# An inverse transform over 64 frequencies as three products of split float32r operands instead of one fp32 product

## The chip, the cores and the metric

The kernel runs on one core of a Trainium2 chip. The metric is the device time of one execution in microseconds; before the change the median of three runs is 1478.95 us (1478.46 to 1480.79).

## The reference

The input x has 8 batches of 2496 rows by 256 features. Each batch goes through a real Fourier transform along the rows, a complex 256 x 256 linear layer with bias, a soft threshold, and the inverse transform. The rows of all batches (19968) then go through a mixture of eight experts, each of which takes exactly 2496 rows, chosen greedily by the order of all logits:

```python
X = np.fft.rfft(x, axis=1);  Xr, Xi = X.real, X.imag
Yr = Xr @ w_r - Xi @ w_i + b_r
Yi = Xr @ w_i + Xi @ w_r + b_i
Y  = soft(Yr, 0.01) + 1j * soft(Yi, 0.01)      # sign(v) * max(|v| - 0.01, 0)
y  = np.fft.irfft(Y, n=2496, axis=1)
# gate: logits = y @ w_gate; pairs (row, expert) in falling order, a row goes to
# the first expert that still has room (2496 rows each)
out[rows of e] = np.maximum(y[rows of e] @ w1[e], 0) @ w2[e]
```

## The kernel before

The transform of length 2496 = 39 x 64 is done in two steps, forward and back. For one batch these are: a transform over 39 points (matmuls of L1168), a change of layout through a scratch tensor T1 in DRAM, the transform over 64 points (L1208), the linear layer (L1227 for the two outputs' own terms, L1235 for the shared one, with the weights as split pairs), bias and soft threshold on VectorE and ScalarE (L1238 to L1246), the inverse over 64 frequencies (L1256), a way through T2 in DRAM, the inverse over 39 (L1294, in the last batch L1287), and the transposes and the gate's products for the logits (L1314, L1336). The frequencies of one batch go in ten groups p = 0 to 9.

Most of the products are made of split operands: a float32 value is rounded to a float32r "high" part and the rest is subtracted out as a "low" part, and high x high, high x low and low x high are summed in PSUM as three float32r products. The inverse over 64 frequencies is one of those that are not: `mm4` (from L1251) multiplies plain fp32. For two groups p at once it does eight matmuls, each over 64 rows (one of the halves i of the partitions, a row tile of TensorE) by 256 columns; the halves write two PSUM tiles `ps4`. In the profile a plain fp32 matmul is two records. Its moving operand is y after the threshold, its weights are the tiles `Gt` (constant cG, 20 blocks of 128 x 128, loaded once at the start).

The tiles live in rings (`RINGS`): a name with so many buffers. y has three (`y1`), the threshold's helper t one (`y2`); after the threshold y lies in `y1` until `mm4` has read it. After the transform stage the same buffers are lent to the experts by the lists `G2` and `GROUPS`: `W`, the experts' split weights, lies in `sp8`, `sh8` and `FG8`.

The order of all instructions is written in advance by a planner (`Plan.run`): every task has an engine, a duration, a place `pos` and the tasks it depends on; the planner plays the work through and gives each engine the task that can start first, with `pos` to decide between tasks that are ready within a small hold time. Constants `Q` shift the places, `SLACK` adds safety to waits, `port=True` marks VectorE and GpSimd tasks that the planner keeps from overlapping. The batches overlap: while one is in its middle, the next is in its first transform and the last in its second.

From the logits of the first four batches VectorE makes the lists of 512 rows for each of eight "early" blocks (`Router.early`), which TensorE starts on while the last batches are still running; the closing rounds (`Router.closing`) then fill up the experts one after the other, and each round's list is needed by the block of 1984 rows that follows (`Experts.run`; L710 first product, L729 and L730 second; L535 writes the list, L657 gathers the rows, L742 scatters the results, L683 writes the split, turned rows).

Of the kernel before, what the change touches and what calls it, by code (L numbers as in the profile page):

```python
# [280 lines left out]
P1X = -8.145  # L281
LATE = dict(sp=1.71, raw=7.61, gather=2.51, scatter=6.24)
SLACK = dict(split=1.661, count=0.243, back=0.303, lists=0.8, os=1.437, hid=0.28, mm4=0, mm4l=0.807, tr=0.477, trl=2.345, gate=0.682, gatel=2.407)
IOTA = True
Q = dict(hV=0.086, hA=0.014, hT=0.054, hP=0.38, e0=43.3, e1=87.756, en=112.714, le=5.187, ge=4.634, c0=1028.809, cs=55.92, c1=1077.612, c1a=1056.826, n0=223.981, n2=109.946, ll=69.251, gs=66.402, gl=3.358, be=14.243, bl=76.075, xp=17.572, f0=8.116, p1=-0.114, p1s=0.45, p57=2.954, p57s=0.337, p5=3.739, p56s=1.261, p5s=0.966, xl=3.918, xs=1.11, m2=0.077, m3=-0.909, zz=2.417, m4=-0.514, l5=4.692, s5=-1.867, w5=1.439, t5=1.266, g5=-3.412, r0=12.442, gb=0.7, gw=0.71, lg=1.866, aa=0.168, ba=3.378, sc=3.601, k2=2.568, xw=1.4, xv=4.054, xv2=2.336, gl2=13.031)
YLV = (1, 5, 7)
SOFT = (2, 3, 4, 5, 6)
# [29 lines left out]
class Kit:  # L317
# [675 lines left out]
def phase_a(K, H, x, w_r, w_i, b_r, b_i, w_gate, cD1, cF, cG, cD5, YD, LG, NB=B):  # L993
# [17 lines left out]
    Gt = [sb("FG8" if b - a > 4 else "FG2", [128, b - a, 128]) for a, b in CUT]  # L1011
# [9 lines left out]
    def dve(n): return 0.068 + n / 960  # L1021
# [51 lines left out]
    def load_weights(after):  # L1073
# [38 lines left out]
    def batch(b):  # L1112
# [22 lines left out]
        if b: T1 = K.dram("T1", [128, 20, 256])  # L1135
        else: Z = [sb(k, [128, 2, b1 - a1, 128]) for k, (a1, b1) in zip(("sp8", "sp8", "xt"), SH)]
# [61 lines left out]
        zs, zd = [], []  # L1198
        for p in range(10):
# [58 lines left out]
            gates['mm4', b, p][0] = plan.add('T', 2.12, pos + Q['m4'], mm4, zs + zd + [BG_[part(GQ, 2 * p)]], list(ps4), uses=[Gt[p // 8]], slack=SLACK['mm4l' if b == NB - 1 else 'mm4'])  # L1258
# [4 lines left out]
            zs, zd = [], []  # L1263
# [84 lines left out]
    last_sh, yt, yq = [], [], []  # L1348
# [7 lines left out]
def fast(tc, nc, H, x, w_r, w_i, b_r, b_i, w_gate, cD1, cF, cG, cD5, YD, LG, w1, w2, cR, out, spectral=True):  # L1356

    RINGS = dict(xt=2, xh=2, xl=2, s1st=3, sh8=4, sh4=2, FG8=2, FG2=2, sp8=2, yr=2, xTh=2, xTl=2, y1=3, y2=1, s4st=2, s2c=3, s2h=2, s2l=2, yst=3, yTh=5, yTl=4, lgst=1,
# [251 lines left out]
```

## Time and profile before

| | |
|---|---|
| median of three runs | 1478.95 us |
| the profiled execution, its span | 1477.74 us, 1475.9 us |
| mean granted TensorE clock | 0.997 of full speed |
| busy of the span: TensorE, VectorE, ScalarE, GpSimd | 98%, 77%, 60%, 36% |
| transfers | 240.50 MB, mean 163 GB/s |
| lines of the inverse over 64 (L1256) | 640 matmul records, 80.6 us |
| of the linear layer (L1227) | 960 matmul records |

A busy share is the time in which the engine has at least one instruction running. TensorE's matmuls overlap, so the sum of their durations is more than the busy time, and how far apart they start tells more of their cost than how long one takes. The transform stage with its tail ends at about 585 us, where the last logits are computed; the experts' products begin at 537 us and run to the end.

### The profile page before, as it was taken

The page shows a single profiled execution, that of the slowest core. Times are in us where ns is not written, and L with a number is a line of the kernel's source. Part 1 is how long each engine was busy: PE and PEld are TensorE (multiplying, and loading weights), DVE is VectorE, ACT ScalarE, POOL GpSimd, SP SyncE. Part 2 cuts the span into 40 slices and gives each one's busy share as a digit, 9 for nine tenths or more (in the row PEclk, how much of TensorE's full clock was granted, in tenths as well). Part 3 has the DMA queues.
Part 4 walks back from the last instruction along what each step waited for, and adds up shares of the span by engine and source line. Part 5 has one row for each costly group of instructions (what it writes and reads, how often), then busy time and mean ns, then how long its engine had stood idle before and what let it go on. Part 6 is the DMA issues. An engine that isn't in the chain of part 4 may idle for free.

```text
span 1475.9 us, 32728 instructions
## 1 busy us (share of the span) xinstructions
PE 1449.2 (98%) x9135; PEld 1221.8 (83%) x9142; DVE 1131.0 (77%) x3234; ACT 888.7 (60%) x2092; POOL 525.2 (36%) x497
## 2 busy tenths in 40 slices
PE   8999999999999999999999999999999999999997
PEld 7888888888888877888878878788888888888886
DVE  6868788875899888899999898997877554553432
ACT  4678999999899786444546363645446542442331
POOL 0013414343432543521444535445453535321112
PEclk9999999999999999999999999999999999999999
DMA  5697869787777656433543536354434334321000
GB/s 199 205 316 247 281 213 293 226 283 231 232 231 251 205 172 193 159 119 104 169 136 110 169 109 180 123 161 138 133 118 141 113 118 143 113 67 42 24 22 30
DMA packets 221994, 240.50 MB, mean 163 GB/s; under 512 B 97598, under 2 KB 183787, under 8 KB 221803
## 3 DMA queue, kind: packets, MB, share of 16 engines
q1 hardware_dynamic: 201833, 180.00, 39.2%
q0 software_dynamic: 19840, 58.22, 12.0%
q8 instruction: 74, 1.21, 0.3%
q14 instruction: 117, 0.96, 0.2%
q10 hardware_dynamic: 130, 0.11, 0.0%
HBM read 139.34 MB, written 98.91 MB: 161 GB/s over the span
## 4 chain that ended last, share of the span: by engine, by line
PE 85%; DVE 7%; ACT 3%; DMA 2%; issue 2%; SPq 1%; POOL 0%; POOLq 0%; DVEq 0%; ACTq 0%
PE b L710 23%; PE b L729 15%; PE b L730 8%; PE b L1227 7%; PE b L1256 5%; PE b L1208 4%; PE b L1235 4%; PE b L1168 3%; PE b L1294 3%; PE pt L710 3%; PE pt L729 2%; PE b L1314 2%; PE pt L730 1%; PE b L732 1%; PE b L1336 1%
## 5 line engine op out<-in xcount | busy, mean ns | idle before, releaser
L1038 POOL TENSOR_TENSOR s2l<-s2c,s2h 120x512 fp32r<-120x512 f32 (+1 forms) x84 | 105.0, 1256 | 257.9 <-ACT s2h L1035 246.9
L1227 PE MATMUL b<-wt,xTh 128*128 128x256 f32 x640 | 128.3, 297 | 0.9 <-ACT xTh L1214 0.9
L742 POOL DMA_INDIRECT out_dram<-xTh,li x64 | 65.2, 1018 | 158.5 <-DVE xTh L739 97.5
L1227 PEld LDWEIGHTS b<-wt,xTh 128*128 128x128 f32 x640 | 103.1, 191 | 6.5 <-issue 1.4
L742 POOL DMA_INDIRECT out_dram<-xTl,li x64 | 66.0, 1032 | 101.8 <-DVE xTl L739 56.9
L1325 POOL TENSOR_TENSOR yTl<-yr,yTh 128x468 bf16<-128x468 f32 (+1 forms) x55 | 61.3, 1115 | 102.5 <-ACT yTh L1321 79.1
L1208 PE MATMUL b<-FG,sh 128*128 128x128 f32 x640 | 92.2, 278 | 1.2 <-DVE sh L1189 1.2
L1227 PE MATMUL b<-wt,xTl 128*128 128x256 f32 x320 | 91.9, 287 | 1.3 <-DVE xTl L1217 1.3
L1208 PEld LDWEIGHTS b<-FG,sh 128*128 128x128 f32 x640 | 82.7, 191 | 6.3 <-issue 2.4
L738 ACT COPY xTh<-b 128x256 f32<-128x256 f32 x66 | 24.7, 374 | 95.2 <-PE b L730 76.6
L1256 PE MATMUL b<-y,FG 64*128 64x256 f32 x640 | 80.6, 390 | 0.1
L1240 DVE TENSOR_TENSOR y<-b,sx 128x512 f32<-128x512 f32 x80 | 54.9, 688 | 27.1 <-ACT sx L1238 24.2
L1256 PEld LDWEIGHTS b<-y,FG 64*128 64x128 f32 x640 | 58.3, 186 | 12.8 <-issue 1.3
L1168 PE MATMUL b<-xh,d 117*120 117x512 f32 (+1 forms) x154 | 64.2, 423 | 2.3 <-ACT xh L1035 2.2
L1294 PE MATMUL b<-s2h,d 120*117 120x512 f32 (+1 forms) x168 | 65.9, 399 | 0.0
L1319 DVE TENSOR_TENSOR yr<-b,yTh 128x468 f32<-128x468 f32 (+1 forms) x88 | 54.8, 625 | 13.9 <-ACT yTh L1318 13.0
L1038 DVE TENSOR_TENSOR xl<-xt,xh 117x512 fp32r<-117x512 f32 (+1 forms) x77 | 56.8, 747 | 11.0 <-ACT xh L1035 10.7
L1235 PE MATMUL b<-wt,xTh 128*128 128x256 f32 x320 | 63.4, 291 | 0.0
L1227 PEld LDWEIGHTS b<-wt,xTl 128*128 128x128 f32 x320 | 60.8, 190 | 3.1 <-DVE xTl L1217 2.7
L634 POOL DMA_INDIRECT xt<-in_moe_w_dram,wi x32 | 33.8, 1055 | 67.6 <-DVE sh L644 20.7
L738 ACT COPY xTl<-b 128x256 f32<-128x256 f32 x68 | 25.4, 373 | 53.8 <-PE b L730 39.9
L739 DVE TENSOR_TENSOR xTh<-b,xTh 128x256 f32<-128x256 f32 x66 | 27.6, 418 | 38.8 <-ACT xTh L738 36.4
(1229 smaller groups left out, 5275.1 us busy)
## 6 DMA issues: line engine op xcount, KB each, us to landing
T<-s4st SPq DMA_DIRECT2D x80, 256.0 KB
s2c<-T SPq DMA_DIRECT2D x80, 240.0 KB
YD<-yst SPq DMA_DIRECT2D x80, 234.0 KB
xt<-in_x_dram SPq DMA_DIRECT2D x35, 512.0 KB
sh<-T SPq DMA_DIRECT2D x35, 512.0 KB
T<-s1st SPq DMA_DIRECT2D x70, 240.0 KB
xt<-in_moe_w_dram SPq DMA_DIRECT2D x32, 512.0 KB
XG<-yTh SPq DMA_DIRECT2D x11, 256.0 KB
```

The lines of the kernel that those rows point to most:

```text
L710: T.matmul(ps.t[:, 0:w], lhsT=W1[m].t[:, a, 128 * ft:128 * ft + 128], rhs=x_.t[:, 0:w], start=q + m == 0, stop=q + m == 3)
L729: T.matmul(ps.t, lhsT=hh.t[:, u:u + 128], rhs=W2[ft // 4].t[:, :, ft % 4], start=ft == 0, stop=False)
L730: T.matmul(ps.t[:, 0], lhsT=hl.t[:, u:u + 128], rhs=w_[0], start=False, stop=ft == 7)
L742: ins = P.indirect_dma_start(out=self.out, out_offset=bass.IndirectOffsetOnAxis(ap=oi.t[0:M, oo + t:oo + t + 1], axis=0), in_=o.t[0:M], in ...
L1038: lambda: eng.tensor_tensor(lb[1](), src(), hb[1](), op=OP.subtract), [srcb, hb[0]], [lb[0]], port=True)
L1168: T.matmul(ps.t[0:M], lhsT=d1[0:k_, a, 0:M], rhs=v.t[0:k_], start=i == 0, stop=i == 2)
L1208: T.matmul(ps.t[:, :, dt, i], lhsT=sh[k // 8].t[:, k % 8, 128 * dt:128 * dt + 128], rhs=at(Ft, k), start=True, stop=True)
L1227: T.matmul(pc.t[:, c], lhsT=a.t[:, 1 - c, dt], rhs=wt[2 - c].t[:, w, dt], start=not pb and dt == 0 and a is th and w == 0, stop=(c == 1 or ...
L1235: T.matmul(pa.t, lhsT=a.t[:, 2, dt], rhs=wt[0].t[:, w, dt], start=dt == 0 and a is th and w == 0, stop=dt == 1 and a is tl)
L1256: T.matmul(ps4[i].t[:, r], lhsT=at(Gt, 2 * (p - 1 + r) + c)[h], rhs=zs[r].t[h, c], start=c == 0, stop=c == 1)
L1294: T.matmul(ps.t[0:M, gs_], lhsT=d5[0:k_, a, 0:M], rhs=v.t[0:k_, gs_], start=i == 0, stop=i == 2)
L1325: yq.append(plan.add('V' if on else 'P', dve(2 * W) if on else pool(2 * W), pos + Q['t5'], lambda yh=yh, yl=yl, yr=yr, W=W, on=on: (V if o ...
```

## The change

In batches 1 to 7 (batch 0 stays in fp32) the value z after the threshold is split on the way: a copy rounds it into `zh` (VectorE, float32r), and a subtraction leaves the rest in `zl` (VectorE for odd p, GpSimd for even p). `mm4x` then does three float32r products, G high x zh, G low x zh and G high x zl, 24 matmuls where there were eight. The constant cG holds G and its two float32r parts side by side, and `load_g` brings the parts in by six transfers from GpSimd's queue in the first batch; the high part takes the two `sp8` tiles, the low part follows in the tiles of the fp32 constant. z is written to `zl`'s ring (batch 0) or in place of t, y's ring has one buffer, and the planner's constants `Q`, `SLACK` and `P1X` have other values throughout.

```diff
-    return dict(cD1=two(D1), cF=Fm.astype(np.float32), cG=G.astype(np.float32), cD5=two(D5))
+    return dict(cD1=two(D1), cF=Fm.astype(np.float32), cG=np.concatenate([G, split(G)[0], split(split(G)[1])[0]], axis=1).astype(np.float32), cD5=two(D5))
...
-P1X = -8.145
+P1X = -9.506
...
+ZLV = (1,)
...
-    Gt = [sb("FG8" if b - a > 4 else "FG2", [128, b - a, 128]) for a, b in CUT]
+    Gt = [sb("G8" if b - a > 4 else "G2", [128, b - a, 128]) for a, b in CUT]
...
+            GH[:] = sb("sp8", [128, 16, 128], F32R), sb("sp8", [128, 8, 256], F32R)
+            GL[:] = sb("G8", [128, 16, 128], F32R), sb("G2", [128, 4, 128], F32R)
...
             y, t, zz = sb("y1", [128, 2, 256]), sb("y2", [128, 2, 256]), vb()
+            z = t if b else sb("zl", [128, 2, 256])
...
-                plan.add('V', dve(512), pos + Q['zz'], lambda y=y, t=t: V.scalar_tensor_tensor(y.t, y.t, 0.0, t.t, op0=OP.min, op1=OP.add), [y, t], [y, zz], port=True)
+                plan.add('V', dve(512), pos + Q['zz'], lambda y=y, t=t, z=z: V.scalar_tensor_tensor(z.t, y.t, 0.0, t.t, op0=OP.min, op1=OP.add), [y, t], [z, zz], port=True)
...
+            if b:
+                zh, zl, zq = plan.buf("zh", lambda s: GH[1].t[:, 2 + 2 * int(s[2:]):4 + 2 * int(s[2:])]), sb("zl", [128, 2, 256], F32R), vb()
+                plan.add('V', dve2(512), pos + Q['zz'], lambda z=z, zh=zh: V.tensor_copy(zh.t, z.t), [zz, BH_[-1]], [zh, zq], uses=[z, GH[1]], port=True)
+                on = p % 2 in ZLV
+                plan.add('V' if on else 'P', dve(512) if on else pool(512), pos + Q['zz'], lambda z=z, zh=zh, zl=zl, on=on: (V if on else P).tensor_tensor(zl.t, z.t, zh.t, op=OP.subtract), [zq], [zl], uses=[z, zh, GH[1]], port=True)
+                z, zz = zl, zl
+                zu.append(zh)
...
+            def mm4x(p=p, zs=zs, zu=zu, ps4=ps4):
+                for r in range(2):
+                    for c in range(2):
+                        k = 2 * (p - 1 + r) + c
+                        for n, (g, z) in enumerate(((ghi(k, 1)[:, 0], zu), (GL[k // 16].t[:, k % 16], zu), (ghi(k, 1)[:, 0], zs))):
+                            for i in range(2):
+                                h = slice(64 * i, 64 * i + 64)
+                                T.matmul(ps4[i].t[:, r], lhsT=g[h], rhs=z[r].t[h, c], start=c == n == 0, stop=c == 1 and n == 2)
...
+        if not b: load_g(ev)
...
+    def load_g(ev):
+        for q, (k0, k1) in enumerate(GQ):
+            G, o = k0 // 16, k0 // 16 * 16
+            add_dma(10 + Q['gs4'], lambda k0=k0, k1=k1: nc.gpsimd.dma_start(ghi(k0, k1 - k0), cG[:, 20 + k0:20 + k1].bitcast(F32R)), 65e3 * (k1 - k0), [], [GH[G], BH_[q]], 'P', after=ev[:1], run=512 * (k1 - k0))
+            add_dma(10 + Q['gs4'], lambda k0=k0, k1=k1, G=G, o=o: nc.gpsimd.dma_start(GL[G].t[:, k0 - o:k1 - o], cG[:, 40 + k0:40 + k1].bitcast(F32R)), 65e3 * (k1 - k0), [], [GL[G], BL_[q]], 'P', after=fg[1], run=512 * (k1 - k0))
...
-    RINGS = dict(... FG8=2, FG2=2, sp8=2, ... y1=3, y2=1, ...
+    RINGS = dict(... FG8=1, FG2=1, G8=1, G2=1, sp8=2, zh=3, ... y1=1, y2=1, zl=2, ...
```

## Rows read from the trace of the kernel before

**Rows 1.** The page: busy us (share) xinstructions, and granted clock in 40 slices

```profile
PE 1449.2 (98%) x9135; PEld 1221.8 (83%) x9142; DVE 1131.0 (77%) x3234; ACT 888.7 (60%) x2092; POOL 525.2 (36%) x497
...
PEclk9999999999999999999999999999999999999999
```

**Rows 2.** The chain of waits from 200 to 300 us: start us, us, what

```profile
by line: PE b L1227 24.3%; PE b L1168 15.2%; PE b L1208 13.8%; PE b L1256 13.5%; PE b L1294 12.5%; PE b L1235 11.4%; PE b L1314 6.5%; PE b L1336 2.9%
...
208.83 1.93 PE b L1256 x16
210.75 1.62 PE b L1227 x12
...
218.96 1.43 PE b L1227 x12
...
250.07 1.93 PE b L1256 x16
```

**Rows 3.** TensorE's waits from 95 to 568 us: us in total, times, longest

```profile
PE pt L471 <- DVE cnt L466: 1.8, 2, 1.1
```

**Rows 4.** Busy time of each engine by stretch, with instructions, clock, transfers

```profile
core 0: us, PE busy (x) PEld busy (x) DVE busy (x) ACT busy (x) POOL busy (x), PEclk, DMA share, GB/s
95.20:568.00 472.80, 466.82 (x3738) 397.95 (x3743) 390.49 (x826) 417.67 (x954) 178.31 (x152) 1.00 0.76 242
421.30:485.70 64.40, 63.51 (x535) 54.62 (x535) 60.93 (x180) 58.99 (x145) 19.20 (x15) 1.00 0.74 240
568.00:706.00 138.00, 138.00 (x784) 113.61 (x783) 125.75 (x420) 69.39 (x170) 43.81 (x42) 1.00 0.38 125
0.00:95.20 95.20, 87.38 (x615) 74.77 (x616) 70.64 (x179) 57.34 (x133) 0.70 (x6) 0.98 0.69 230
```

**Rows 5.** Line L1256 (ns min/median/max), and one task of it in the timeline

```profile
L1256 PE MATMUL b<-y,FG x640: 376/376/480, 37.7 to 531.3; 64*128 64x256 f32 x160
...
250.00 2.00 PE L1256 MATMUL b<-y,FG 64*128 64x256 f32 x16
...
250.00 1.60 PEld L1256 LDWEIGHTS b<-y,FG 64*128 64x128 f32 x16
...
250.00 0.19 PEld L1256 LDWEIGHTS b<-y,FG 64*128 64x128 f32 x2
```

**Rows 6.** Lines of the nearest operations: ns min/median/max, first and last start, forms

```profile
L1245 DVE TENSOR_SCALAR y<-y x30: 394/421/1400, 31.4 to 528.3; 128x512 f32<-128x512 f32 x30
...
L1246 DVE TENSOR_TENSOR y<-y,y x30: 675/688/1751, 32.3 to 528.7; 128x512 f32<-128x512 f32 x30
...
L1038 POOL TENSOR_TENSOR s2l<-s2c,s2h x84: 727/1284/1754, 96.8 to 535.8; 120x512 fp32r<-120x512 f32 x70, 120x256 fp32r<-120x256 f32 x7, 40x256 fp32r<-40x256 f32 x7
...
L1038 DVE TENSOR_TENSOR xl<-xt,xh x77: 674/684/1766, 25.6 to 427.1; 117x512 fp32r<-117x512 f32 x70, 78x512 fp32r<-78x512 f32 x7
...
L1218 DVE TENSOR_TENSOR xTl<-sx,xTh x80: 402/417/1514, 26.5 to 523.7; 128x256 fp32r<-128x256 f32 x80
```

**Rows 7.** VectorE and GpSimd in the timeline around 245 us: start us, us

```profile
244.26 0.69 DVE L1229 TENSOR_TENSOR b<-b,bf 128x512 f32<-128x512 f32 x1
244.86 0.42 DVE L1215 TENSOR_TENSOR sx<-b,sx 128x256 f32<-128x256 f32 x1
...
246.39 1.08 DVE L1218 TENSOR_TENSOR xTl<-sx,xTh 128x256 fp32r<-128x256 f32 x1
...
246.11 1.08 POOL L1325 TENSOR_TENSOR yTl<-yr,yTh 128x468 bf16<-128x468 f32 x1
```

**Rows 8.** Groups by line and shape, 0 to 1050 us: busy us, mean ns of one

```profile
L1038 DVE TENSOR_TENSOR xl<-xt,xh 117x512 fp32r<-117x512 f32 x70 | 52.0, 753 | 9.5 <-ACT xh L1035 9.5
...
L1218 DVE TENSOR_TENSOR xTl<-sx,xTh 128x256 fp32r<-128x256 f32 x80 | 40.7, 509 | 0.7 <-ACT xTh L1216 0.5
```

**Rows 9.** The first closing expert in the timeline: list's waiter, its rows, first product

```profile
706.47 0.98 POOL L742 DMA_INDIRECT out_dram<-xTh,eoi  x1 [3.29 <-DVE li L535]
...
736.38 0.68 DVE L683 TENSOR_TENSOR s2l<-yTl,FG 128x512 fp32r<-128x512 f32 x1
...
745.59 0.40 PE L710 MATMUL b<-s1st,sp 128*128 128x512 f32 x1
```

More of the change, by code (lines that the diff above doesn't have):

```diff
@@ L280 @@
 UX = 6
[L281 removed]
+P1X = -9.506
 LATE = dict(sp=1.71, raw=7.61, gather=2.51, scatter=6.24)
[L283 removed]
+SLACK = dict(split=1.232, count=0.28, back=0.343, lists=0.657, os=2.117, hid=0.956, mm4=0.318, mm4l=0.855, tr=0.555, trl=2.378, gate=0.645, gatel=2.461)
 IOTA = True
[L285 removed]
+Q = dict(hV=0.085, hA=0.009, hT=0.041, hP=0.322, e0=45.966, e1=88.74, en=107.337, le=8.978, ge=-3.041, c0=1027.621, cs=56.794, c1=1078.68, c1a=1064.524, n0=191.639, n2=95.971, ll=48.387, gs=72.789, gl=2.94, be=14.728, bl=69.672, xp=19.043, f0=8.429, p1=-0.156, p1s=0.45, p57=1.995, p57s=1.281, p5=3.533, p56s=1.457, p5s=0.966, xl=4.239, xs=0.81, m2=-0.131, m3=-0.467, zz=1.197, m4=-3.175, l5=5.748, s5=-1.157, w5=1.781, t5=1.367, g5=-1.587, r0=11.753, gb=0.7, gw=0.71, lg=1.288, aa=0.264, ba=2.517, sc=2.914, k2=2.829, xw=4.354, xv=3.181, xv2=1.704, gl2=12.612, gs4=0.482)
 YLV = (1, 5, 7)
+ZLV = (1,)
 SOFT = (2, 3, 4, 5, 6)
@@ L1078, in load_weights @@
         for i, w in enumerate((w_r, w_i)):
-            st = sb("y1", [128, 2, 256])
+            st = sb("y2" if i else "y1", [128, 2, 256])
             sw.append(st)
@@ L1135, in batch @@
         if b: T1 = K.dram("T1", [128, 20, 256])
-        else: Z = [sb(k, [128, 2, b1 - a1, 128]) for k, (a1, b1) in zip(("sp8", "sp8", "xt"), SH)]
+        else:
+            Z = [sb(k, [128, 2, b1 - a1, 128]) for k, (a1, b1) in zip(("sp8", "sp8", "xt"), SH)]
+            GH[:] = sb("sp8", [128, 16, 128], F32R), sb("sp8", [128, 8, 256], F32R)
+            GL[:] = sb("G8", [128, 16, 128], F32R), sb("G2", [128, 4, 128], F32R)
         for u in range(NU):
@@ L1197, in batch @@
         T2 = K.dram("T2", [128, 20, 256])
-        zs, zd = [], []
+        zs, zd, zu = [], [], []
         for p in range(10):
@@ L1256, in mm4 @@
                             T.matmul(ps4[i].t[:, r], lhsT=at(Gt, 2 * (p - 1 + r) + c)[h], rhs=zs[r].t[h, c], start=c == 0, stop=c == 1)
+            def mm4x(p=p, zs=zs, zu=zu, ps4=ps4):
[6 more added lines that the diff above has]
+                                T.matmul(ps4[i].t[:, r], lhsT=g[h], rhs=z[r].t[h, c], start=c == n == 0, stop=c == 1 and n == 2)
             gates['mm4', b, p] = [0]
-            gates['mm4', b, p][0] = plan.add('T', 2.12, pos + Q['m4'], mm4, zs + zd + [BG_[part(GQ, 2 * p)]], list(ps4), uses=[Gt[p // 8]], slack=SLACK['mm4l' if b == NB - 1 else 'mm4'])
+            gates['mm4', b, p][0] = plan.add('T', 1.5 if b else 2.12, pos + Q['m4'], mm4x if b else mm4, zs + zd + zu + [X[part(GQ, 2 * p)] for X in ((BH_, BL_) if b else (BG_,))], list(ps4), uses=[GL[p // 8], GH[p // 8], GH[1]] if b else [Gt[p // 8]], slack=SLACK['mm4l' if b == NB - 1 else 'mm4'])
             for i in range(2):
@@ L1346, in batch, with ghi @@
             ys = []
-    last_sh, yt, yq = [], [], []
+    last_sh, yt, yq, GH, GL = [], [], [], [], []
+    BH_, BL_ = [vb() for _ in GQ], [vb() for _ in GQ]
+    def ghi(k, n):
+        return GH[0].t[:, k:k + n] if k < 16 else GH[1].t[:, k // 2 - 8:(k + n + 1) // 2 - 8].rearrange("p a (c m) -> p (a c) m", c=2)[:, k % 2:k % 2 + n]
+    def load_g(ev):
[3 more added lines that the diff above has]
+            add_dma(10 + Q['gs4'], lambda k0=k0, k1=k1, G=G, o=o: nc.gpsimd.dma_start(GL[G].t[:, k0 - o:k1 - o], cG[:, 40 + k0:40 + k1].bitcast(F32R)), 65e3 * (k1 - k0), [], [GL[G], BL_[q]], 'P', after=fg[1], run=512 * (k1 - k0))
     head, wl, fg = [], [], []
```

14 lines of the change are left out of this document (7 added, 7 removed).

## The prediction, made before the result was known

> **What bounds the kernel now.** I read the page first, then the chain of waits in one stretch, then TensorE's waits, then the busy times by stretch. On the page TensorE is busy 98% of the span at full clock, VectorE 77% [rows 1]. A busy share alone doesn't say that an engine is the bound, so the chain comes next: between 200 and 300 us every link of it is TensorE, with no other engine and no transfer in it [rows 2]. The list of waits agrees: from 95 to 568 us, the seven batches that the change touches and the first expert work, TensorE's largest wait for another engine sums to 1.8 us [rows 3]. So a microsecond taken off TensorE there is a microsecond off the kernel, as long as something else is not late. What would be late next is read from the same stretch: VectorE is busy 390.5 of 472.8 us, ScalarE 417.7, GpSimd 178.3, and in its fullest batch (421.3 to 485.7) VectorE was busy 60.9 of 64.4 us, 95% [rows 4].
>
> **TensorE: eight steps become twelve shorter ones.** One task of the inverse (two frequencies' pairs) is now 8 matmuls, each recorded as two, so 16 records, and in the chain it costs 1.93 us each time; the twelve L1227 matmuls behind it take 1.62 us where they take 1.43 elsewhere, so some 0.19 us more for the change of row tiling and back [rows 2]. That part stays, as the new products use the same two 64-row tiles. The records go in pairs, one in each half of the rows: the timeline has two weight loads within 0.19 us, as long as one. The first pair starts at 250.00 and waits about 0.10 for weights (480 against 376 ns), the last begins at 252.00 - 0.38 = 251.62, so the seven steps between take (251.62 - 250.10) / 7 = 0.217 us each [rows 5]. Eight steps are 1.74 us.
>
> The new task has 24 matmuls, three for each of the eight, all float32r over 256 columns: twelve pairs. No row of before has a float32r pair in two row tiles. The nearest is float32r of the same 256 columns over all rows: twelve L1227 in 1.43 us, 0.12 each [rows 2]. If a pair again costs what one costs, twelve are 1.44 us, and a task gains 0.30 (0.296 unrounded). Seven batches have five tasks each: 35 x 0.296 = 10.4 us; I use 10.2, as the rows are rounded. Bounds: at best a step is half of the present one (0.108), which gives 1.30 per task and 35 x 0.44 = 15.4 us; at worst the halves don't pair in float32r, 24 x 0.12 = 2.88, and the change costs 35 x 1.14 = 40 us. I take 0.12, as the pairing in the trace is one of tiles, not of a data type.
>
> The row first: sixteen weight loads of 64 x 128 were issued within 1.60 us, two at a time [rows 5]. The Trainium skill ("TensorE: Matmul & The Clock Gate", LDWEIGHTS (loading the stationary operand)) says that a load's time goes by its columns, not its rows, about 107 ns for 128. By that alone, one load after the other, 24 loads would be 2.57 us by estimate, and the change would lose (rival D). The Trainium skill ("TensorEngine Tiling (Array Packing)", Key Properties) lets different tiles load in parallel, and the trace agrees with that one.
>
> **VectorE and GpSimd: the two new passes.** Per frequency pair p there is now a copy of z to its rounded half (VectorE) and a subtraction that gives the rest, on VectorE for odd p and on GpSimd for even p. So each of the 35 tasks adds two copies and one subtraction to VectorE, and one subtraction to GpSimd. The nearest copy is L1245, 512 elements in SBUF with one operand, 421 ns; the subtraction is L1246, 688 ns, and on GpSimd L1038, 1284 ns [rows 6]. On a filled VectorE the next instruction starts before the last has ended: from 244.26 to 244.86, 0.60 us after one of 0.69 [rows 7]. I take 0.08 off each: 2 x 0.34 + 0.61 = 1.29, times 35 = 45 us on VectorE (from both sides: 33 if a copy took half as long, 54 with the full durations) and 35 x 1.28 = 45 us on GpSimd, which goes from 178 to 223 of 472 and has room.
>
> A second cost comes with it. VectorE's L1218 at 246.39 took 1.08 us instead of 0.417, and ended just after GpSimd's L1325, which ran from 246.11 to 247.19 [rows 6, 7]: an operation with both inputs in SBUF waited for GpSimd. The means show its size: L1218 509 against 417 ns, 80 times, and L1038 on VectorE 753 against 684, 70 times: 7.4 + 4.8 = 12.2 us [rows 6, 8], 15% of their 81 us. With a quarter more GpSimd work, these rise by some 3 us, and the new 54 us of VectorE operations, all between SBUF tiles, pay 15% x 1.25, 10 us: 13 us more (0 if the written order keeps them apart, 25 if it is twice as bad). The Trainium skill ("SBUF — State Buffer", Who interferes with whom) calls this an exclusive lock that also holds for copies in the two-port mode; the trace agrees for two SBUF inputs, and L1245 (maximum 1400 ns) fits for one. By that lock the other way round GpSimd too would wait for the copies, which moves nothing, as it has room.
>
> **What is late next.** VectorE's work from 95.2 to 568 becomes 390.5 + 45 + 13 = 448.5 us. TensorE would need 472.8 - 10.2 = 462.6 us for it; that is a VectorE filled to 97%. The fullest batch reached 95% with TensorE hardly waiting [rows 3, 4]. At 95% the stretch takes 472.1, at 94% 477.1, at 93% 482.3 us. VectorE does not hold each batch back at once, since the routing of the early experts is loose work that slides. Where the delay comes due is the first closing expert: its list is there by 706.47, its gathered rows, turned and split, at 736.38 + 0.68 = 737.06, and its first product runs at 745.59 [rows 9], 8.5 us of margin, with VectorE 91% busy from 568 to 706 [rows 4]. TensorE comes 10.2 us earlier, the rows come L later or earlier than now, so TensorE waits max(0, 1.7 + L). Later closings have more.
>
> I take a fill of 94.5%, a little under what the fullest batch had: 474.6 us, L = 1.8, wait 3.5, net 10.2 - 3.5 = 6.7 us.
>
> **What I cost at nothing.** The two more copies of the inverse's constants are 40 x 64 KB = 2.6 MB over six GpSimd issues: at the 230 GB/s of 0 to 95.2, 11 us of transfers, in a stretch where the transfers' engines are 69% busy and GpSimd works 0.7 us [rows 4]; they must be there at the second batch's first task, at 95 us. Uncovered, up to 11 us. z, now kept in two more buffers while y keeps one: the buffers' count is the same, and TensorE's task waits for a subtraction 1.7 us later than before. Behind it in TensorE's order stand other products of the same and the next batch, whose evictions all engines wait for; the order is written for it, so nothing, and at worst one wait like the longest now (1.1 us, rows 3) at each task, 38 us. The planner's constants are all moved, and with them the order of everything: TensorE waits so little that a better order has some 2 us to give [rows 3], and a worse one is priced in C. The first expert's weights lose two tiles that were free since the first batch: these now hold constants until the last task (529 us); two to four splits later, TensorE has the last batch's tail to do. Nothing, up to 5 us.
>
> **The sum.** 1477.74 us for the profiled execution (span 1475.9 and 1.84 around it) less 6.7 is 1471.0; the median of the runs lies 1.2 above the profiled one, so 1478.95 - 6.7 = **1472 us**.
>
> **Rivals.**
> A, all of it arrives: VectorE fills to 97% or GpSimd's lock costs nothing, so no wait at the first closing expert: 1478.95 - 10.2 = 1469, and 1463.5 with the step of 0.108. For it: 95% was reached with TensorE untouched. Against: only in one batch, with routing work that nobody waited for.
> B, VectorE takes it all back: fill 93% gives L = 9.5, wait 11.2, net -1: 1480, no change.
> C, slower: VectorE becomes the bound of the seven batches. The point is a fill of 92.6% (L = 11.5, net -3). At 92%, 487.5 us, L = 14.7, wait 16.4: net -6.2, 1485; at 91%, 1490. For it: over the whole stretch VectorE is at 83% now. Against: in most of that stretch it waits because TensorE hands it nothing.
> D, the change doesn't do what it says on TensorE: float32r in two row tiles doesn't pair, matmuls or loads come one after the other, +40 us, 1519. Only a missing row speaks for it; the paired loads speak against.
>
> **How the numbers follow.** The forecast (net 3 to 9.5) has 0.41, A 0.17, B 0.15, C 0.23, D 0.04. A measurement of this kernel can tell about 0.2% (3 us) from no change: faster 0.41 + 0.17 = 0.58, same 0.15, slower 0.27. The forecast's own range is 1469.5 to 1476. For 8 in 10 I go from A's lower end, 1463, to C at 91.5%, 1487; outside lie D and the worst of C and of the uncovered waits.
>
> **What would show it.** Right: a task of the inverse at 1.60 to 1.68 us in the chain (1.93 now), its loads still two at a time; VectorE busy 93% or more from batch 2 to 7; a TensorE wait of a few us around the first closing expert, or a list that comes before 706. Wrong: a task near 3 us (D); VectorE's new copies far from 0.34 to 0.42 us; TensorE waiting for the new subtraction at every task; or idle VectorE together with an unchanged time.

## The result: slower by 1.4%

The changed kernel takes 1499.63 us (median of 4 runs, 1496.98 to 1501.41), the kernel before 1478.7 beside it: 1.0138 times as long (95% interval 1.0119 to 1.0157). The prediction was 1472, range 1463 to 1487; the slower side is what happened, and by more than rival C priced it. The profiled execution took 1499.81 us with a span of 1498.0, 22.1 more than before. Lines are a few numbers higher than before: the inverse's product is L1277 (L1256 before), the new copy L1254, the new subtraction L1256, the linear layer L1231 and L1239, its input's low parts (xTl) L1221 and L1222.

From the page of the changed kernel, to compare with [rows 1]: busy times, VectorE's slices, the clock's slices, and the engines' shares of the chain that ended last (for each instruction, followed back, what released it):

```profile
PE 1448.8 (97%) x9418; PEld 1227.7 (82%) x9422; DVE 1196.0 (80%) x3339; ACT 886.9 (59%) x2092; POOL 589.8 (39%) x538
...
DVE  6869998988899999899999889989877655554431
...
PEclk9999999999999989999999999999999999999999
...
PE 80%; DVE 13%; ACT 3%; issue 2%; DMA 1%; POOL 0%; SPq 0%; POOLq 0%; DVEq 0%; ACTq 0%
```

The busy shares alone hardly differ. In the chain, though, VectorE's share is twice that of the kernel before:

```profile
PE 85%; DVE 7%; ACT 3%; DMA 2%; issue 2%; SPq 1%; POOL 0%; POOLq 0%; DVEq 0%; ACTq 0%
```

Where the time went is seen in one stretch, from the second batch's first task of the inverse to the last product of the logits. Its busy times by engine (as [rows 4]), in the kernel before:

```profile
95.20:585.10 489.90, 483.92 (x3868) 410.95 (x3875) 406.07 (x877) 427.02 (x987) 186.38 (x159) 1.00 0.75 240
```

and in the changed kernel:

```profile
100.80:609.40 508.60, 481.15 (x4142) 414.02 (x4146) 465.66 (x979) 426.95 (x992) 238.52 (x193) 0.99 0.74 229
```

The stretch starts 5.6 us later, is 18.7 us longer, and 2.2 us come back behind it: 22.1. TensorE's busy time falls by 2.8 us only, and its idle time (the stretch less the first number, PE) rises from 6.0 to 27.5. VectorE rises from 406.1 to 465.7, 83% to 91.6%.

TensorE's waits from 100 to 600 us in the changed kernel (total, times, longest), the six largest, to compare with [rows 3], where the largest was 1.8:

```profile
PE b L1231 <- DVE xTl L1221: 7.0, 7, 1.7
PE pt L811 <- DVE rng L888: 4.9, 1, 4.9
PE b L1172 <- DVE xl L1039: 2.7, 5, 0.8
PE b L1239 <- DVE xTl L1222: 2.6, 4, 1.1
PE b L1277 <- DVE sp L1254: 2.2, 1, 2.2
PE b L1316 <- DVE cnt L466: 1.9, 1, 1.9
```

All six end with VectorE, but hardly any with the new passes: TensorE waits mostly for older work (xTl, xl, the lists) that now comes later in VectorE's order. The waits are not spread evenly. The stretch in five parts (columns as above):

```profile
100.80:280.00 179.20, 172.20 (x1499) 151.87 (x1500) 165.45 (x289) 154.78 (x342) 81.66 (x63) 1.00 0.80 248
280.00:400.00 120.00, 119.84 (x1074) 106.17 (x1075) 101.16 (x176) 111.02 (x246) 66.81 (x54) 1.00 0.84 262
400.00:490.00 90.00, 79.88 (x674) 68.98 (x672) 88.51 (x256) 72.06 (x165) 33.27 (x27) 0.98 0.60 190
490.00:540.00 50.00, 49.98 (x470) 45.14 (x471) 48.28 (x107) 38.81 (x97) 26.41 (x21) 1.00 0.51 157
540.00:609.40 69.40, 59.25 (x440) 41.85 (x438) 62.26 (x156) 50.28 (x146) 30.36 (x30) 0.93 0.74 222
```

TensorE is idle 7.0 us, 0.2, 10.1, 0.0 and 10.2, with VectorE busy 92%, 84%, 98%, 97% and 90%. So a full VectorE does not by itself stop TensorE; which pass is late, and what waits for it, must count too. How one wait comes about is seen around 271 to 277 us, here ordered by cause:

```profile
270.82 1.36 POOL L1347 TENSOR_TENSOR yTl<-yr,yTh 128x468 bf16<-128x468 f32 x1 [3.80 <-ACT yTh L1343]
271.16 1.57 DVE L1256 TENSOR_TENSOR zl<-y,sp 128x512 fp32r<-128x512 f32 x1
272.76 0.73 ACT L1247 ACTIVATE y<-y,ml 128x512 f32<-128x512 f32 x1 [0.57 <-DVE zl L1256]
...
275.59 1.22 POOL L1347 TENSOR_TENSOR yTl<-yr,yTh 128x468 bf16<-128x468 f32 x1 [1.72 <-ACT yTh L1343]
275.80 1.29 DVE L1222 TENSOR_TENSOR xTl<-sx,xTh 128x256 fp32r<-128x256 f32 x1
277.15 0.39 PE L1239 MATMUL b<-wt,xTl 128*128 128x256 f32 x1 [1.06 <-DVE xTl L1222]
```

The new subtraction takes 1.57 us in place of 0.68, as GpSimd's L1347 runs until 272.18. ScalarE's next threshold (L1247) waits 0.57 us for it. ScalarE's later work, xTh among it, stands behind that, and VectorE's xTl, made from xTh, is itself held by the next L1347 of GpSimd and takes 1.29 us in place of 0.42. TensorE then waits 1.06 us. The chain that ended last runs through all of these VectorE passes, where it stayed on TensorE for 100 us on end before [rows 2]. The Trainium skill ("SBUF — State Buffer", Who interferes with whom) calls the hold an exclusive lock; the trace agrees.

The largest single wait, 4.9 us from 548 to 553, is neither for xTl nor for a new pass. Ahead of rng in VectorE's order stand two passes of the experts' weights' split (L645, median 0.68 us each), which took 5.90 us together while four passes of GpSimd ran:

```profile
547.07 5.90 DVE L645 TENSOR_TENSOR sh<-xt,sh 128x512 fp32r<-128x512 f32 x2
547.26 2.12 POOL L1347 TENSOR_TENSOR yTl<-yr,yTh 128x468 bf16<-128x468 f32 x2
549.32 2.48 POOL L1039 TENSOR_TENSOR s2l<-s2c,s2h 120x512 fp32r<-120x512 f32 x2
```

### The profile page after: what moved, and what is told of

It is laid out like the page before. It is cut to its first block, busy times and chain, and to the rows that moved or that the text cites. A ratio compares the mean times of both kernels' runs of the same rounds, so it can differ in the third digit from the quotient of the medians.

```text
span 1498.0 us, 33534 instructions
## 1 busy us (share of the span) xinstructions
PE 1448.8 (97%) x9418; PEld 1227.7 (82%) x9422; DVE 1196.0 (80%) x3339; ACT 886.9 (59%) x2092; POOL 589.8 (39%) x538
## 4 chain that ended last, share of the span: by engine, by line
PE 80%; DVE 13%; ACT 3%; issue 2%; DMA 1%; POOL 0%; SPq 0%; POOLq 0%; DVEq 0%; ACTq 0%
PE b L711 24%; PE b L730 16%; PE b L731 8%; PE b L1231 5%; PE pt L711 4%; PE b L1212 3%; PE b L1239 3%; PE b L1277 2%; PE b L1172 2%; PE b L1316 2%; PE pt L730 2%; PE b L1336 1%; PE pt L731 1%; DVE xTl L1221 1%; PE b L733 1%
## 5 line engine op out<-in xcount | busy, mean ns | idle before, releaser
L1039 POOL TENSOR_TENSOR s2l<-s2c,s2h 120x512 fp32r<-120x512 f32 (+1 forms) x84 | 105.9, 1269 | 79.5 <-ACT s2h L1036 73.9
L1231 PE MATMUL b<-wt,xTh 128*128 128x256 f32 x640 | 128.3, 297 | 0.5 <-ACT yst L1318 0.5
L1231 PEld LDWEIGHTS b<-wt,xTh 128*128 128x128 f32 x640 | 102.4, 190 | 4.8 <-ACT yst L1318 0.7
L1231 PE MATMUL b<-wt,xTl 128*128 128x256 f32 x320 | 92.2, 288 | 7.9 <-DVE xTl L1221 7.7
L1256 POOL TENSOR_TENSOR zl<-y,sp 128x512 fp32r<-128x512 f32 x35 | 49.2, 1407 | 114.8 <-DVE sp L1254 76.8
L1347 POOL TENSOR_TENSOR yTl<-yr,yTh 128x468 bf16<-128x468 f32 (+1 forms) x55 | 65.6, 1195 | 68.6 <-ACT yTh L1343 58.8
L1039 DVE TENSOR_TENSOR xl<-xt,xh 117x512 fp32r<-117x512 f32 (+1 forms) x77 | 60.7, 795 | 15.1 <-ACT xh L1036 14.6
L1231 PEld LDWEIGHTS b<-wt,xTl 128*128 128x128 f32 x320 | 60.7, 190 | 11.1 <-DVE xTl L1221 10.8
L574 ACT ACTIVATE ajunk<-b,h_bs 128x156 bf16<-128x156 f32 x117 | 46.1, 394 | 30.6 <-PE b L569 27.0
L1239 PE MATMUL b<-wt,xTh 128*128 128x256 f32 x320 | 63.4, 290 | 0.0
L1245 DVE TENSOR_TENSOR y<-b,sx 128x512 f32<-128x512 f32 x80 | 54.6, 682 | 10.2 <-ACT sx L1242 9.0
L1318 ACT COPY yst<-b 117x512 f32<-117x512 f32 (+2 forms) x96 | 52.7, 558 | 7.8 <-PE b L1316 5.8
```

The source lines that it names most:

```text
L1039: lambda: eng.tensor_tensor(lb[1](), src(), hb[1](), op=OP.subtract), [srcb, hb[0]], [lb[0]], port=True)
L1231: T.matmul(pc.t[:, c], lhsT=a.t[:, 1 - c, dt], rhs=wt[2 - c].t[:, w, dt], start=not pb and dt == 0 and a is th and w == 0, stop=(c == 1 or ...
L1239: T.matmul(pa.t, lhsT=a.t[:, 2, dt], rhs=wt[0].t[:, w, dt], start=dt == 0 and a is th and w == 0, stop=dt == 1 and a is tl)
L1347: yq.append(plan.add('V' if on else 'P', dve(2 * W) if on else pool(2 * W), pos + Q['t5'], lambda yh=yh, yl=yl, yr=yr, W=W, on=on: (V if o ...
```

## The experiments

All were timed in three rounds beside the kernel before. "Split" means the 70 copies and 70 subtractions, "products" the three float32r products. The table gives the time, its ratio to before, and from the windows of each profile the stretch above: its length, TensorE's idle time in it, and VectorE's share.

| | us | ratio (95%) | stretch | PE idle | DVE |
|---|---|---|---|---|---|
| before | 1478.7 | | 489.9 | 6.0 | 82.9% |
| e1 products only | 1476.63 | 0.9987 (0.9977–0.9996) | 484.5 | 10.3 | 85.1% |
| e12 products, copies | 1477.66 | 0.9994 (0.9985–1.0004) | 486.9 | 10.5 | 87.0% |
| after | 1499.63 | 1.0138 (1.0119–1.0157) | 508.6 | 27.5 | 91.6% |
| e2 split, plain product | 1508.39 | 1.0209 (1.0192–1.0226) | 518.2 | 23.6 | 90.9% |
| e13 split, two products | 1492.68 | 1.0101 (1.0084–1.0118) | 499.0 | 28.1 | 92.9% |
| e14 subtraction not awaited | 1498.57 | 1.0133 (1.0116–1.0151) | 507.5 | 23.9 | 91.2% |
| e15 a ScalarE copy in its place | 1497.59 | 1.0127 (1.0110–1.0145) | 502.2 | 21.8 | 86.4% |
| e18 two buffers for z | 1495.89 | 1.0126 (1.0107–1.0146) | 505.6 | 23.6 | 91.2% |
| e5 subtractions on GpSimd | 1493.22 | 1.0086 (1.0065–1.0107) | 503.3 | 19.2 | 87.9% |
| e9 subtractions on VectorE | 1501.97 | 1.0152 (1.0134–1.0169) | 506.9 | 21.0 | 94.1% |
| e20 batches 6, 7 plain | 1494.25 | 1.0110 (1.0082–1.0139) | 501.4 | 23.3 | 89.4% |

**TensorE's part alone (e1).** The threshold writes float32r, and that tile is the operand of all three products.

```diff
-            z = t if b else sb("zl", [128, 2, 256])
+            z = sb("zl", [128, 2, 256], F32R if b else F32)
...
-                zh, zl, zq = plan.buf("zh", lambda s: GH[1].t[:, 2 + 2 * int(s[2:]):4 + 2 * int(s[2:])]), sb("zl", [128, 2, 256], F32R), vb()
...
-                plan.add('V' if on else 'P', dve(512) if on else pool(512), pos + Q['zz'], lambda z=z, zh=zh, zl=zl, on=on: (V if on else P).tensor_tensor(zl.t, z.t, zh.t, op=OP.subtract), [zq], [zl], uses=[z, zh, GH[1]], port=True)
-                z, zz = zl, zl
-                zu.append(zh)
+                zu.append(z)
```

> The changed kernel without the split of z: the threshold writes float32r straight into zl's buffer and that one operand serves all three products, so TensorE has the 24 matmuls and VectorE and GpSimd have neither the 70 copies nor the 70 subtractions (the low part of z is left out of the computation and the high part counted for it). Theory A, VectorE sets the pace of the seven batches: without its 45 us the kernel keeps the ten that TensorE gains, 1464 to 1474 us, last logits before 585 us. Theory B, the new order of work (all planner constants moved) is what costs: still 1490 or more. Theory C, y in one buffer instead of three ties the engines together: still 1485 or more, as y's ring stays at one here.

1476.63: theories B and C of this run fall, and A is missed by 2.6. Some 10 us were to be won, and 2 came; the first task stands at 102.5 us, 7.3 later than before, and from there to the last logits 5.4 are won back.

**VectorE's and GpSimd's part alone (e2).**

```diff
...
-                        for n, (g, z) in enumerate(((ghi(k, 1)[:, 0], zu), (GL[k // 16].t[:, k % 16], zu), (ghi(k, 1)[:, 0], zs))):
...
+                            T.matmul(ps4[i].t[:, r], lhsT=ghi(k, 1)[:, 0][h].bitcast(F32), rhs=zs[r].t[h, c].bitcast(F32), start=c == 0, stop=c == 1)
...
```

The subtractions become additions here, and the planner is told 2.12 us for the task, as in the kernel before.

> The changed kernel with all of the copies and subtractions (as additions, so that what is left is z doubled) but with the plain fp32 product of eight matmuls, of G's high part. The low part of G is left out. TensorE's task is 1.93 us again. Theory A: VectorE sets the pace, so TensorE's ten us more hardly matter: 1497 to 1506. Theory B or C, TensorE still the bound with waits added: ten us more than the changed kernel, 1507 to 1515.

1508.39, in the range of theories B or C: 8.8 over the changed kernel for about 10 us more on TensorE. So the split costs the time, yet TensorE's own time still counts: VectorE isn't simply the bound.

**The order (e3, e4, e7, e16).** e3 is the kernel before with the new constants, e4 the changed kernel with the old ones; e7 tells the planner the task's real length, e16 moves one constant.

```diff
-P1X = -8.145
+P1X = -9.506
# e3, with Q and SLACK of the changed kernel; e4 the reverse, gs4 kept
-            gates['mm4', b, p][0] = plan.add('T', 1.5 if b else 2.12, ...
+            gates['mm4', b, p][0] = plan.add('T', 1.82 if b else 2.12, ...
# e7
-P1X = -9.506
+P1X = -9.3
# e16
```

> The kernel before with the planner constants Q, SLACK and P1X of the changed one, nothing else. Theory A: the constants only move the order a little, 1474 to 1486. Theory B: they are what costs, 1490 or more. Theory C: 1474 to 1486.

> The changed kernel with the planner constants Q, SLACK and P1X of the one before. Theory A: VectorE has as much to do, 1494 to 1512. Theory B: the gain appears, 1464 to 1476. Theory C: 1490 to 1505.

> The changed kernel with the planner told 1.82 us for a task of the inverse (1.63 in the chain and 0.19 for the tiling) instead of 1.5. Theory A: the order changes a little, VectorE has the same work, 1494 to 1504. Theory P, the order is bad because it is written for a TensorE that is faster than the real one: 1490 or less.

> The changed kernel with one of the planner's constants moved by 2% (P1X from -9.506 to -9.3) and nothing else: the same work in a slightly different order. It measures how far an order as such moves the time. If orders near each other are alike: 1496 to 1503. If the written order is a lottery: anything from 1490 to 1530, and then differences of that size between the other runs prove nothing on their own.

e3 1480.55 (ratio 1.0013, 1.0004 to 1.0023); e4 1533.43 (1.0381, 1.0364 to 1.0398), above all three expectations; e7 1499.26 (1.0127, 1.0097 to 1.0156); e16 1499.69 (1.0143, 1.0125 to 1.0161). The new constants cost the old kernel 2 us and save the new one 34; the two neighbouring orders tried (e7, e16) are alike, but a badly fitting one costs more than the whole change.

**Shifting VectorE's work (e5, e9, e6, e8).** All subtractions on GpSimd, all on VectorE, the bias by a matmul in place of VectorE's addition, the copies on ScalarE.

```diff
-ZLV = (1,)
+ZLV = ()
# e5; e9: (0, 1)
-BV = (0, 2, 3, 4)
+BV = (0,)
# e6
-                plan.add('V', dve2(512), pos + Q['zz'], lambda z=z, zh=zh: V.tensor_copy(zh.t, z.t), [zz, BH_[-1]], [zh, zq], uses=[z, GH[1]], port=True)
+                plan.add('A', act(512, False), pos + Q['zz'], lambda z=z, zh=zh: A.copy(zh.t, z.t), [zz, BH_[-1]], [zh, zq], uses=[z, GH[1]])
# e8
```

> The changed kernel with all 70 subtractions of the low part on GpSimd. VectorE loses 35 of them (21 us at 0.60 each), GpSimd gets 45 us more. Theory A, VectorE's load as such sets the pace: 1484 to 1493. Theory L, VectorE loses its time by waiting for GpSimd's operations on shared tiles: 1500 or more, as there are more of these to wait for.

> The changed kernel with all 70 subtractions on VectorE. VectorE gets 21 us more, GpSimd loses 45. Theory A: 1508 to 1520. Theory L: 1497 or less.

> The changed kernel with the bias of batches 2, 3 and 4 added by a matmul of ones, as in batches 1, 5, 6 and 7, instead of by VectorE: 30 additions of 0.60 us less there (18 us), 30 matmuls of 0.23 us more (7 us). Theory A: if batches 2 to 4 are held back by VectorE, 1484 to 1494. Theory M, that what costs lies in the batches with routing work (5 to 7) alone, or TensorE sets the pace in 2 to 4: 1497 to 1507.

> The changed kernel with the 70 copies on ScalarE instead of VectorE: VectorE 24 us less in the seven batches, ScalarE some 36 us more (it was busy 418 of 473 us before). Theory S (VectorE's occupied time decides): 1488 to 1495. Rival N (ScalarE, now over 90% full, is as late as VectorE was): 1498 or more.

1493.22, 1501.97, 1494.65 (1.0114, 1.0095 to 1.0133) and 1496.07 (1.0117, 1.0100 to 1.0134): some 20 us off VectorE, or on, move the time by -6 to +2. e5, e6 and e8 end just over the first theory's range, e9 hits neither of its two. A VectorE that bound the stretch by itself would have given back nearly all of it.

**Two reliefs together (e11, e17).** e17 is e5 and e6 in one; e11 also has the edit of e7.

> The changed kernel with three edits together: all subtractions on GpSimd, the linear layer's bias by a matmul in all batches but one, and the planner's task at 1.82 us. Theory S: the two reliefs of VectorE add up (-6.4 and -5.0 against the changed kernel), 1485 to 1491. Rival O (both relieve the same few full batches, so only one of them counts): 1491 to 1496. In either case it stays slower than the kernel before (1479).

> The changed kernel with all subtractions on GpSimd and the bias by a matmul, the planner's task at 1.5 us as in the changed kernel. Together with the task at 1.82 us this took 1514.6. If the planner's cost made that order bad: 1484 to 1493, the two single gains together or the larger of them. If the two edits don't go together: 1505 or more.

1514.58 (1.0246, 1.0224 to 1.0268) and 1500.70 (1.0143, 1.0122 to 1.0164): both worse than either relief alone, e17 between its two expectations. The reliefs don't add up. In e11 VectorE is busy 86% of the time from 90 us to the last logits (86% in e17, 91% in the changed kernel), and it is the slowest of the six; that the planner's constants fit neither is likely after e4, but wasn't shown.

**Copies against subtractions (e12).**

```diff
...
-                on = p % 2 in ZLV
-                plan.add('V' if on else 'P', dve(512) if on else pool(512), pos + Q['zz'], lambda z=z, zh=zh, zl=zl, on=on: (V if on else P).tensor_tensor(zl.t, z.t, zh.t, op=OP.subtract), [zq], [zl], uses=[z, zh, GH[1]], port=True)
-                z, zz = zl, zl
+                z, zz = zh, zh
```

> The changed kernel with the 70 copies, but without the 70 subtractions: the rounded copy is the operand of all three products (the low part of z is left out). TensorE's work is that of the changed kernel; VectorE keeps 24 of its 45 us more, GpSimd's 45 us and their mutual waiting go. Theory S (the cost follows VectorE's occupied time, waiting for GpSimd included): of the 23 us between products alone (1476.6) and the changed kernel (1499.6) the copies keep about 24 of 24 + 21 + 22 parts, so 1483 to 1488. Rival G (GpSimd's subtractions and the waiting they cause are the whole cost): 1475 to 1481. Rival K (one more link in each batch's chain before the product is what costs, and the copy is that link): 1491 or more.

1477.66: theories S (the cost follows VectorE's occupied time) and K fall. The time lies in the range of rival G, GpSimd's subtractions; but e9, which has none on GpSimd, is as slow as the changed kernel, so G falls there. 70 copies cost 1 us, the 70 subtractions 22. Its stretch, with the columns as above:

```profile
102.50:589.40 486.90, 476.45 (x4155) 411.88 (x4156) 423.68 (x956) 426.49 (x996) 193.85 (x161) 1.00 0.77 240
```

VectorE at 87% leaves TensorE 10.5 us idle, and TensorE's wait for xTl is

```profile
PE b L1231 <- DVE xTl L1221: 1.3, 3, 0.6
```

where the changed kernel has 7.0. Between the two kernels with the same work on TensorE lie 17.0 us of idle time and 4.7 of busy time (481.15 - 476.45), most of it the clock's (last section): 21.7 in the stretch. With e12 divided into the same five parts, 6.8 of the 17.0 lie before 280 us, 6.0 between 400 and 490, and 4.1 behind that.

**TensorE lighter under the whole split (e13).**

```diff
-                        for n, (g, z) in enumerate(((ghi(k, 1)[:, 0], zu), (GL[k // 16].t[:, k % 16], zu), (ghi(k, 1)[:, 0], zs))):
+                        for n, (g, z) in enumerate(((ghi(k, 1)[:, 0], zu), (GL[k // 16].t[:, k % 16], zu))):
```

> The changed kernel with all copies and subtractions and their waits, but only two of the three products (G high times the low part of z is left out): per task 8 steps of 0.12 us in place of 12, 35 x 0.48 = 17 us less on TensorE; VectorE and GpSimd as in the changed kernel. Theory T (TensorE's time still counts in full, VectorE's passes only open gaps beside it, as the plain product over the same passes suggested with +8.8 us for about 10): 1480 to 1487. Rival V (VectorE with GpSimd is the bound of the seven batches, TensorE's time hardly counts below the present one): 1494 to 1500. Between them, 1487 to 1494: both bind in turn.

1492.68, between the two (the planner is told 1.0 us for the task here): 17 us less on TensorE give 7. Both bind in turn.

**The subtraction's wait, or its work (e14, e15).** e14 awaits none of them, e15 puts a copy on ScalarE in their place.

```diff
-                z, zz = zl, zl
+                z, zz = zh, zh
# e14
...
+                plan.add('A', act(512, False), pos + Q['zz'], lambda z=z, zl=zl: A.copy(zl.t, z.t), [zq], [zl], uses=[z, GH[1]])
# e15
```

> The changed kernel with all copies and all subtractions done, but the third product reads the rounded copy, so that TensorE waits for no subtraction (the low part of z is left out of the sum). Theory W (the work on VectorE and GpSimd and their waiting for each other cost the 22 us): 1493 to 1503, as the changed kernel. Rival L (the later link before the product costs it): 1475 to 1483, as with the copies only. Between them: both.

> The changed kernel with each subtraction replaced by a copy of z to the low part's tile on ScalarE (the low part isn't computed): TensorE still waits for a pass behind the first copy, but VectorE has 21 us and GpSimd 45 us less, and nothing new takes their shared port but the copies. ScalarE has some 36 us more, which alone cost nothing when the first copies were put there (1496.1 against 1499.6). Theory W: 1475 to 1485. Rival L: 1492 to 1502.

e14 1498.57: the cost is there without the wait. e15 1497.59, where theory W wanted 1475 to 1485 and rival L 1492 to 1502: it is there without the work on VectorE and GpSimd, too. No run puts ScalarE's copy in and does not await it, so in e15 the wait and ScalarE's own time are not parted. e15's stretch:

```profile
100.50:602.70 502.20, 480.42 (x4138) 412.92 (x4139) 434.14 (x959) 455.39 (x1061) 196.96 (x164) 0.99 0.74 232
```

Here ScalarE is the full one (455.4 of 502.2, 91%; 87.6% in e12), and TensorE waits for VectorE's xTl as in the changed kernel:

```profile
PE b L1231 <- DVE xTl L1221: 7.2, 9, 1.8
```

xTl is the difference of what ScalarE evicts and rounds (xTh) one step earlier; that a full ScalarE delays it as a full VectorE does is seen in one wait only, at 513.17 (1.58 us), where the chain runs through the new copy. In the longest, at 527.27, it runs through a VectorE pass (L645) that took 3.72 us beside GpSimd's.

**One buffer (e18), and the last batches (e20).**

```diff
-            y, t, zz = sb("y1", [128, 2, 256]), sb("y2", [128, 2, 256]), vb()
+            y, t, zz = sb("y1", [128, 2, 256]), sb("yz" if b else "y2", [128, 2, 256]), vb()
...
-    GROUPS = dict(W=(8, slots("sp8", "sh8", "FG8", "G8")), raw=(2, slots("xt")), xg=(10, G2), xw=(5, G2), xf=(2, G2), hid=(20, G2), xT=(8, G2), os=(8, slots("xTh", "xTl")),
+    GROUPS = dict(yz=(2, ["y20", "FG20"]), W=(8, slots("sp8", "sh8", "FG8", "G8")), raw=(2, slots("xt")), xg=(10, G2), xw=(5, G2), xf=(2, G2), hid=(20, G2), xT=(8, G2), os=(8, slots("xTh", "xTl")),
# e18
-            z = t if b else sb("zl", [128, 2, 256])
+            z = t if 0 < b < 6 else sb("zl", [128, 2, 256])
...
-            if b:
+            if 0 < b < 6:
...
+            def mm4h(p=p, zs=zs, ps4=ps4):
+                for r in range(2):
+                    for c in range(2):
+                        for i in range(2):
+                            h = slice(64 * i, 64 * i + 64)
+                            T.matmul(ps4[i].t[:, r], lhsT=ghi(2 * (p - 1 + r) + c, 1)[:, 0][h].bitcast(F32), rhs=zs[r].t[h, c], start=c == 0, stop=c == 1)
...
# e20
```

> The changed kernel with two buffers for t and z in batches 1 to 7 (the second one is a tile that lies idle between the first batch and the experts). All passes, waits and products as in the changed kernel. Rival R (the next threshold waits for the one buffer until the subtraction has read it, and the linear layer's products behind it): 1476 to 1487. Theory W (the passes' own time on engines that are full, wherever they are put): 1494 to 1502.

> The changed kernel in batches 1 to 5; in batches 6 and 7 no copy, no subtraction, and one plain fp32 product with the high part of G (the low part of G is left out there). TensorE has 10 x 0.30 = 3 us more than in the changed kernel. If the cost of the passes lies in the last, fullest batches (most of the 22 us arise after 490 us, where the distance to the kernel with the copies only grows from 5 to 20 us): 1482 to 1489. If it lies on all batches alike, two sevenths of 22 us less and 3 more: 1493 to 1499.

1495.89: 3.7 of 22 us at most are the buffer's. 1494.25, in the range for a cost that lies on all batches alike, though the waits themselves fall unevenly (the five parts above).

**What is settled and what isn't.** It is the second set of 70 passes that costs, about 0.3 us for each, on whichever engine it lands; not the products, the copies, the wait by itself, the new constants by themselves or the last batches, and the buffer only little. By which share of each engine it turns into TensorE's idle time stays open: VectorE's share doesn't order the table (e5 and e15 have VectorE about as full as e12 and are 16 and 20 us slower). Nor does any run show whether an order fitted further to the split would hide the passes: after the 34 us of e4, that rival stands. No complete version beats the kernel before; e1 and e12 lie within 0.2% of it, and only by leaving a part out.

## Why the prediction was wrong

**TensorE's task: right.** In the chain it costs 1.63 us where 1.60 to 1.68 was forecast (1.93 in [rows 2]), and the L1231 products behind it cost 1.62 as before:

```profile
299.91 1.63 PE b L1277 x24
301.54 1.62 PE b L1231 x12
```

The pairs start 0.12 apart in the timeline:

```profile
327.06 0.28 PE L1277 MATMUL b<-sp,G 64*128 64x256 f32 x2
...
327.18 0.28 PE L1277 MATMUL b<-zl,sp 64*128 64x256 f32 x2
...
327.30 0.28 PE L1277 MATMUL b<-sp,sp 64*128 64x256 f32 x2
```

Rival D fell, and with it the estimate of 2.57 us, one load after the other, by the Trainium skill's rule for loads ("TensorE: Matmul & The Clock Gate", LDWEIGHTS (loading the stationary operand)). Two weight loads still run at a time:

```profile
327.06 0.19 PEld L1277 LDWEIGHTS b<-zl,sp 64*128 64x128 f32 x2
```

In e1 and e12 TensorE's busy time in the stretch is 9.7 and 7.5 us less than before, against 10.2.

**VectorE's and GpSimd's work: right.** The groups of the new lines from 90 to 620 us (busy us, mean ns):

```profile
L1256 POOL TENSOR_TENSOR zl<-y,sp 128x512 fp32r<-128x512 f32 x35 | 49.2, 1407 | 114.8 <-DVE sp L1254 76.8 <-PE b L1231 11.0 <-PE b L1239 10.5
...
L1254 DVE CAST sp<-y 128x512 fp32r<-128x512 f32 x70 | 34.2, 489 | 0.2
...
L1256 DVE TENSOR_TENSOR zl<-y,sp 128x512 fp32r<-128x512 f32 x35 | 26.6, 760 | 0.1
```

VectorE has 59.6 us more in the stretch; 45 + 13 = 58 was forecast, the mutual waiting included.

**The constants' loads at nothing: most likely wrong, by 5.6 us.** The transfer share of the first 30 us rises from 65% to 82%, and two of the low part's loads go out at 69.46, in a stretch (60 to 101 us) where the share is 92% in the kernel before and 93% in the changed one. At 79.70 ScalarE's copy had waited 3.69 us for a transfer of the scratch tensor to free its tile, and TensorE 2.75 us for ScalarE behind it:

```profile
69.46 1.06 POOL L1380 DMA_DIRECT2D G<-cG  x2 [34.74 <-PE b L1268]
...
79.70 1.29 ACT L1174 COPY s1st<-b 120x512 f32<-120x512 f32 x2 [3.69 <-DMA T<-s1st]
```

The second batch's first task runs at 100.8 us, not 95.2. It isn't the new order (e3 has it at 95.4) and not the split (e1 and e12, which load the same constants, have it at 102.5; all runs of the table but the kernel before have it between 97.8 and 103.1). An order can move it, too: e4, with the old constants, has it at 113.9. The loads and the changed rings of buffers are what these have in common; no run parted the two or left the loads out.

**The step that failed:** "I take a fill of 94.5%, a little under what the fullest batch had", and the reason before it, "VectorE does not hold each batch back at once, since the routing of the early experts is loose work that slides". VectorE reached 91.6%. For this stretch, with the measured 465.7 us, 94.5% would have made 492.8; it was 508.6, so this step is 15.8 us, some 4 of them by the clock (last section). One full batch [rows 4] was taken as proof that all can be so, and a fill as what sets the time. The five parts in the section on the result say otherwise: from 490 to 540 us VectorE is 97% full and TensorE never idle, up to 280 it is 92% full and TensorE loses 7.0 us. And the routing wasn't loose. From 400 to 490 us, the part with the most of it, TensorE loses 10.1 us (2.0 in the kernel before), and the longest wait for xTl has routing passes (L462, L520) right ahead of it in VectorE's order; in the chain (start us, us, what), with TensorE's wait from the timeline:

```profile
432.49 1.70 DVE junk L462 x8
434.18 0.59 DVE cno L520
434.77 0.33 DVE sx L1219
435.11 0.61 DVE xTl L1221
...
435.76 0.39 PE L1231 MATMUL b<-wt,xTl 128*128 128x256 f32 x1 [1.73 <-DVE xTl L1221]
```

**The margin at the first closing expert: never used.** Its list came at 728 instead of 706, its first product at 766.1 instead of 745.6 [rows 9]; TensorE was late itself by then and did not wait there, so that margin hid nothing, and the forecast's 3.5 us of waiting at this place did not come. TensorE's direct waits for the new passes, a sign that was named for being wrong, came to 2.8 us in all.

**Rival C** named an engine and the sign. By its formula the measured 91.6% gives 448.5 / 0.916 = 489.6, L = 16.8, wait 18.5, net -8.3: 1487. It lacked the 5.6 us before the stretch and the clock, and it let the delay come due only at the closing expert, behind 8.5 us of margin; it came due long before, in single waits from 100.8 us on. And VectorE alone is too narrow a name: e15 is as slow with VectorE at 86% and ScalarE at 91%.

## What to carry to other kernels

Where the bound engine is fed by several engines in a fixed order, work moved from it to them need not be paid evenly: here the first 70 passes cost 1 us and the next 70 cost 22. Before trading, ask which product waits for the queue that gets the new passes and what stands in it behind them; one full stretch without waits doesn't show that all stretches can be so full, and a share of busy time doesn't say where the waits fall. Do the parts of such a change one by one: products, copies and subtractions had quite different prices, and a kernel's written order has to be fitted again to each.

## What the runs showed of the hardware

TensorE's clock fell after its own waits, from full to half speed (2.4 to 1.2 GHz), and the work right behind them took up to twice as long. After the wait at 79.8 us a product of 512 columns takes 0.78 us, twice the usual 0.39 (granted clock 0.50 from 82.5 to 86 us). After a wait of 2.16 us for L1254, which ended at 546.06, and one of 0.65 the float32r pairs start 0.21 apart in place of 0.12:

```profile
82.53 0.78 PE L1172 MATMUL b<-xh,d 117*120 117x512 f32 x1 [2.75 <-ACT xh L1036]
```

```profile
547.59 0.42 PE L1277 MATMUL b<-sp 64*128 64x256 f32 x2
547.80 0.42 PE L1277 MATMUL b<-sp,G 64*128 64x256 f32 x2
548.01 0.42 PE L1277 MATMUL b<-zl,sp 64*128 64x256 f32 x2
```

Inside the stretch from 100.8 to 609.4 us the clock was at half speed twice (columns as [rows 4]):

```profile
437.60:440.60 3.00, 3.00 (x28) 2.77 (x26) 3.00 (x11) 1.68 (x4) 0.69 (x1) 0.50 0.39 111
546.90:556.60 9.70, 4.48 (x21) 3.46 (x22) 8.53 (x15) 4.10 (x12) 5.84 (x6) 0.50 0.48 135
```

Half of the 7.5 us that TensorE was busy there, some 4 us by estimate, is the clock's price.

float32r matmuls of 64 rows in two row tiles pair: 0.12 us per pair of 256 columns, what one of all rows costs [rows 2], with two weight loads at a time. And the VectorE passes of one input can be held by GpSimd too: the copy takes 489 ns in the mean against a median of 416, and its longest, 1495, lies beside GpSimd's L1039:

```profile
215.02 1.27 POOL L1039 TENSOR_TENSOR s2l<-s2c,s2h 120x512 fp32r<-120x512 f32 x1 [3.12 <-ACT s2h L1036]
215.08 1.50 DVE L1254 CAST sp<-y 128x512 fp32r<-128x512 f32 x1
```
